# Transposing put-off probabilities two trios at a time, and filling TensorE's early gaps for longer

## The chip, the cores and the metric

The kernel runs on one core of one Trainium2 chip. The metric is the device time of one execution in microseconds (us). It ran three times before the change; the median is the time before. A profile of one further execution gives the trace: the start and length of every instruction on each engine, and the clock that was granted to TensorE.

## The reference

Two layers, one after the other, in float32. First, causal attention with a sliding window of 128 positions and a linear distance bias, for 8 batches and 8 heads of 576 positions and 64 features; then a gated feed-forward layer over all 4608 tokens.

```python
scores = scale * np.matmul(q, k.transpose(0, 1, 3, 2))
mask = (rel >= 0) & (rel < window)          # rel: query position - key position
scores = np.where(mask, scores + bias[None], -1000000000.0)
scores = scores - np.max(scores, axis=-1, keepdims=True)
attn = np.exp(scores)
attn = attn / (np.sum(attn, axis=-1, keepdims=True) + 1e-09)
out = np.matmul(attn, v)
...
gate = 1.0 / (1.0 + np.exp(-(x @ w_gate)))   # x: 4608 x 512, w_gate: 512 x 1536
val = x @ w_val
return gate * val @ w_out                    # 1536 x 512
```

## The kernel before, in words

**Stages.** From 0 to about 296 us the kernel computes attention and, mixed into it, the gate and value products of the first 3072 tokens for four of the twelve feature chunks ("the stream", line 659). From 296 to about 700 us come the other gate and value products (line 793), and after that the output product (line 927).

**Units, blocks, runs, trios.** Attention is cut into 32 units, each a batch and a pair of heads. A unit has nine blocks of 128 rows. `scores` (line 430 and after) takes a run of eight blocks (four in the first units), which may straddle two units. Its matmuls (line 459) write score banks in PSUM. VectorE then puts masked parts in place (476) and does bias and row minimum (484), and ACT the exponentials with their sums (488). Three blocks make a trio. `probabilities` finishes a trio: POOL adds the small constant to the sums (561), VectorE takes reciprocals (563), VectorE or ACT scale the three blocks (566, 567), TensorE transposes them (573) into one of two work banks, ACT or VectorE copy that bank out (205, 206), and POOL makes two selections out of it into the unit's tile `pt` (584).

**What is put off.** For units from the ninth on (`VHEAD`), a trio that ends in a run isn't finished there: it goes on the list `put_off` and is handed to `probabilities`, one trio after the other, in the next run, behind that run's scores. A run leaves two or three trios. `split_values` multiplies `pt` with the values (line 530) in two halves, one ahead of a run's scores and one behind; both halves use both work banks (`WORK`, banks 6 and 7), and copies out of them to `xt` follow. `work()` hands out the two work banks by turns.

**The order of the work.** Every piece is put into a graph with its engine, a cost, what it reads and writes, and a due time (`want`). `Graph.order` then plans all engines: of the pieces whose inputs are planned, it takes the one that can start first; between equal starts, the one that is due first. The stream has a due time of a million, so it goes wherever nothing else can start. Each engine then has its instructions in planned order, for good. The planner charges LAT on top of a cost before a result may be used (0.25 for TensorE, 0.2 for ACT), SLACK 0.1 ahead of put-off transposes, SWITCH / 2 = 0.18 where TensorE changes the kind of matmul, and STAY 0.4 for leaving attention's kind after time 30.

**Fillers.** Where the plan leaves TensorE idle before time `WARM`, the planner notes how many filler matmuls fit, and `warm` (line 290) multiplies the identity with itself that often, into a bank that nothing reads then. Each filler is two matmul records in the trace.

```python
if o.eng == "PE" and o.start < WARM:
    gap = (o.start - free["PE"] - 0.2) // (0.25 if free["PE"] > 5.0 else 0.45)
```

## Time and profile before

| what | value |
|---|---|
| median of 3 runs | 963.4 us (963.06 to 966.7) |
| the profiled execution | 963.38 us |
| its span, first to last instruction | 961.6 us |
| mean granted TensorE clock | 0.998 |
| TensorE busy in the span | 954.6 us, 6634 matmuls |
| transposes, line 573 | 288 matmuls, 216 + 36 + 36 in three groups |
| fillers, line 290 | 62 matmuls, 10.1 us |
| stream, line 659 | 576 matmuls, 157.1 us |

The profile names engines PE (TensorE matmuls), PEld (its weight loads), DVE (VectorE), ACT (ScalarE), POOL (GpSimd) and SP (which starts DMAs). L573 is line 573 of the kernel before. Matmuls are pipelined, so the length of one overlaps that of the next; distances between starts, and the chain of waits, tell what a group costs. A row of the timeline gives start, length, engine, line, operation, tiles and count, and in brackets the idle time before it with what ended it. A row of the chain gives start, length, and what. A row of windows gives the window and its length, then busy time and number of instructions for PE, PEld, DVE, ACT and POOL, and at the end the granted clock, the DMA share and GB/s.

### The profile page before, as it was taken

The numbers are of one execution on the slowest core, as the hardware profiler recorded it, in microseconds if no ns is written. First come the engines' busy times: TensorE is split into PE (matmuls) and PEld (weight loads), VectorE is DVE, ScalarE is ACT, GpSimd is POOL, SyncE is SP. The second block draws the span as 40 slices with busy tenths as digits, with TensorE's granted clock in tenths as the row PEclk, the third lists the DMA queues.
The fourth block names the chain that finished last, engine by engine and source line by source line (L and its number), as shares of the span: only waits on it lengthen the run. The fifth ranks groups of instructions, "written<-read, shape, count | busy, mean of one in ns | idle before, by whom it ended". The sixth has DMA issues, their size and how long they took to land.

```text
span 961.6 us, 18712 instructions
## 1 busy us (share of the span) xinstructions
PE 954.6 (99%) x6634; PEld 833.6 (87%) x6634; DVE 763.8 (79%) x1893; ACT 517.7 (54%) x1341; POOL 143.2 (15%) x316
## 2 busy tenths in 40 slices
PE   9999999999999999999999999999999999999998
PEld 7678888888889999999988888888888888889998
DVE  8999788788898899878976775674597878877783
ACT  8998788878876354434533543442343433333341
POOL 3545345444441000000000000000000000000000
PEclk9999999999999999999999999999999999999999
DMA  8787778867654344335573473379856254352601
GB/s 308 262 285 251 239 250 290 283 203 244 230 198 163 121 153 136 101 143 192 182 286 116 155 284 134 140 288 347 311 190 207 100 169 159 96 167 88 189 25 50
DMA packets 82653, 186.03 MB, mean 193 GB/s; under 512 B 7808, under 2 KB 36864, under 8 KB 82560
## 3 DMA queue, kind: packets, MB, share of 16 engines
q1 hardware_dynamic: 82416, 184.71, 56.3%
q8 instruction: 52, 0.85, 0.4%
q14 instruction: 41, 0.34, 0.1%
q10 hardware_dynamic: 144, 0.13, 0.1%
HBM read 121.90 MB, written 62.91 MB: 192 GB/s over the span
## 4 chain that ended last, share of the span: by engine, by line
PE 97%; DVE 2%; ACT 0%; issue 0%; POOL 0%; POOLq 0%; DVEq 0%
PE mm L793 42%; PE mm L927 27%; PE mm L659 15%; PE mm L459 5%; PE mm L530 4%; PE mm L573 3%; PE mm L611 1%; PE mm L290 1%; DVE pb L484 0%; DVE pb L566 0%; DVE mm L476 0%; ACT pb L488 0%; DVE first L214 0%; DVE wbits L352 0%; DVE st L563 0%
## 5 line engine op out<-in xcount | busy, mean ns | idle before, releaser
L793 PE MATMUL mm<-xc,w2s 128*128 128x384 f32 (+1 forms) x2016 | 403.8, 362 | 0.0
L793 PEld LDWEIGHTS mm<-xc,w2s 128*128 128x128 f32 x2016 | 363.7, 188 | 39.7 <-DVE later_hs L800 0.5
L927 PE MATMUL mm<-duo,wo 128*128 128x512 f32 (+1 forms) x1260 | 258.9, 367 | 0.0
L927 PEld LDWEIGHTS mm<-duo,wo 128*128 128x128 f32 x1260 | 229.4, 188 | 29.5
L659 PE MATMUL mm<-first,first 128*128 128x512 f32 x576 | 157.1, 409 | 0.1
L659 PEld LDWEIGHTS mm<-first,first 128*128 128x128 f32 x576 | 101.9, 190 | 21.5 <-issue 1.1
L804 ACT ACTIVATE sg<-mm 128x384 f32<-128x384 f32 (+1 forms) x96 | 52.2, 545 | 111.5 <-PE mm L793 63.1
L800 DVE TENSOR_TENSOR mm<-mm,low 128x384 f32<-128x384 f32 (+1 forms) x96 | 60.3, 629 | 60.9 <-PE mm L793 60.1
L205 ACT COPY low<-mm 128x512 f32<-128x512 f32 (+1 forms) x93 | 49.6, 536 | 78.5 <-PE mm L793 66.7
L488 ACT ACTIVATE pb<-pb,st 128x128 f32<-128x128 f32 x216 | 84.6, 397 | 2.1 <-DVE st L484 1.9
L584 POOL TENSOR_SCALAR_AFFINE_SELECT pt<-early_h 128x384 f32<-128x384 f32 x96 | 51.3, 553 | 57.0 <-ACT early_h L205 56.6
L584 POOL TENSOR_SCALAR_AFFINE_SELECT pt<-spread 128x384 f32<-128x384 f32 x96 | 52.3, 567 | 44.0 <-ACT spread L205 43.7
L476 DVE COPY_PREDICATED mm<-early_h,mm 128x256 f32<-128x256 int32 (+1 forms) x144 | 48.8, 389 | 4.1 <-PE mm L459 4.1
L530 PEld LDWEIGHTS mm<-pt,vr 64*64 64x64 f32 x1056 | 43.1, 133 | 10.0 <-issue 5.0
L484 DVE CUSTOM_DVE_ANT_0 pb<-mm,early_h 128x128 f32<-128x128 f32 x216 | 49.6, 282 | 0.0
L530 PE MATMUL mm<-pt,vr 64*64 64x192 f32 (+2 forms) x1056 | 47.3, 284 | 0.0
L566 DVE TENSOR_SCALAR pb<-pb,st 128x128 f32<-128x128 f32 x169 | 42.1, 296 | 1.3
L488 ACT ACTIVATION_READ_ACCUMULATOR pb<-pb,st 128x1 f32 x216 | 41.8, 193 | 0.0
L808 DVE SCALAR_TENSOR_TENSOR later_hs<-sg,later_hs 128x384 f32<-128x384 f32 (+1 forms) x48 | 30.1, 628 | 13.8 <-ACT sg L804 13.6
L205 ACT CAST duo<-csum 128x1024 fp32r<-128x1024 f32 (+1 forms) x26 | 25.2, 969 | 29.0 <-PE mm L927 13.2
L205 ACT COPY early_h<-mm 128x384 f32<-128x384 f32 (+3 forms) x75 | 32.1, 444 | 14.0 <-PE mm L530 8.6
L800 DVE TENSOR_TENSOR later_hs<-mm,later_hs 128x384 f32<-128x384 f32 (+1 forms) x48 | 29.8, 620 | 11.9 <-ACT sg L804 6.5
(144 smaller groups left out, 1202.0 us busy)
## 6 DMA issues: line engine op xcount, KB each, us to landing
hid<-later_hs SPq DMA_DIRECT2D x24, 512.0 KB, 3.8
wo<-stash_o SPq DMA_DIRECT2D x12, 896.0 KB, 7.4
vr<-in_v_dram SPq DMA_DIRECT2D x32, 288.0 KB, 5.0
hid<-later_hs SPq DMA_DIRECT2D x24, 384.0 KB, 2.9
stash_o<-wtmp SPq DMA_DIRECT2D x12, 768.0 KB, 3.5
wraw<-in_moe_w_gate_dram SPq DMA_DIRECT2D x14, 512.0 KB, 5.0
wraw<-in_moe_w_val_dram SPq DMA_DIRECT2D x14, 512.0 KB, 4.1
kr<-in_k_dram SPq DMA_DIRECT2D x11, 576.0 KB, 5.1
```

Of the source, the lines that this page charges most:

```text
L205: g.add("ACT", act_cost(n, psum), lambda: nc.scalar.copy(out(), src()), reads, writes, want, release=release, slack=slack, ways=[("DVE", d ...
L459: nc.tensor.matmul(to, qraw(u)[rows, i // 2, h * D:(h + 1) * D], keys, start=True, stop=True)
L476: g.add("DVE", dve_cost((a1 - a0) * P, psum=True), lambda b=b, a0=a0, a1=a1: nc.vector.copy_predicated(quads(b)[:, a0:a1, 1:3], before[:, ...
L484: g.add("DVE", 0.21, lambda: nc.vector.tensor_tensor_reduce(pb()[:, e], sp[b][:, a, D:D + P], relm[u.p][:, w], op0=ALU.add, op1=ALU.min, s ...
L488: g.add("ACT", 0.39, lambda: nc.scalar.activation(pb()[:, e], pb()[:, e], AF.Exp, bias=st()[:, e:e + 1], scale=-1.0, accum_out=st()[:, 3 + ...
L530: nc.tensor.matmul(mm[WORK[h]][e * D:(e + 1) * D, a - e * S - cuts[h]:b - e * S - cuts[h]], vraw(u)[r * D:r * D + D, c], seen, start=first ...
L584: nc.gpsimd.affine_select(pt(u)[:, f0:f0 + 2 * n - 1:2, :], both(), [[0, n], step], cmp, 0.0, base=0, channel_multiplier=mult)
L659: nc.tensor.matmul(mm[s][:, 0:wd], w.tile(kind, wi, i)[:, c * P:(c + 1) * P], xpart(x, c)[:, 0:wd], start=(k == 0 and c == 0), stop=(k == ...
L793: nc.tensor.matmul(mm[b][:, 0:N2], w.tile2(i, wp)[:, wk, c * P:(c + 1) * P], combo(k, xp, N2)[:, c], start=(start and c == 0 and j == 0), ...
L800: g.add("DVE", dve_cost(N2, psum=True), lambda: nc.vector.tensor_tensor(o(), bk(b)(), a(), op=ALU.add), [("mm", b), *reads] if okeys else ...
L804: g.add("ACT", act_cost(N2, psum=True), lambda: nc.scalar.activation(sg[h](), bk(b)(), AF.Tanh, scale=0.5), [("mm", b)], [("sg", h)], F)
L927: nc.tensor.matmul(mm[b][:, 0:N2], wo2(2 * q + m, wp)[:, k, j * P:(j + 1) * P], duo(xp)[:, m], start=(k in (0, 3, 1) and q == 0 and m == 0 ...
```

## The change

Two edits. First, `probabilities` takes a list of trios. Put-off trios are handed to it two at a time (a third one alone). For each trio the sums, reciprocals and scaling are put into the graph as before; then there is one TensorE piece for all transposes of the list, which reads all its scaled blocks and writes one work bank per trio, so for two trios both of them; its due time is that of the first trio. Then come the copy and the two selections of each trio. Trios that aren't put off go through the same function alone. Second, the time limit `WARM` of the fillers goes from 30 to 45, and they also end with the first matmul of the stream; the limit of 30 in STAY's condition stays, now called `EAGER`.

```diff
--- before.py
+++ after.py
@@ -60,7 +60,7 @@
 W1, WSTEP1 = 0.0, 6.0
 WW, WWSTEP = 28.0, 2.0
 SWITCH = 0.36
-WARM = 30.0
+EAGER, WARM = 30.0, 45.0
 LATE = 4.0
 LATEX = 0.0
 LAND = 4.0
@@ -122,6 +122,7 @@
         free["PE"] = 1.5
         wait = []
         port = moved = 0.0
+        streams = False
         mode = 0
         for o in self.ops:
             if not o.left:
@@ -134,7 +135,7 @@
                 for k, way in enumerate(o.ways):
                     e, cost, lat, shared, emit = way
                     s = max(free[e], o.ready, port if shared else 0.0)
-                    leave = STAY if e == "PE" and mode == 1 and o.mode != 1 and s > WARM else 0.0
+                    leave = STAY if e == "PE" and mode == 1 and o.mode != 1 and s > EAGER else 0.0
                     key = (s + cost - least + leave + (YIELD[e] if k else 0.0), o.want, o.seq)
                     if best is None or key < best[0]:
                         best = key, o, way, s
@@ -142,7 +143,8 @@
             if o.eng == "PE" and o.mode != mode:
                 mode = o.mode
                 o.start += SWITCH / 2
-            if o.eng == "PE" and o.start < WARM:
+            streams = streams or o.eng == "PE" and o.want == 1.0e6
+            if o.eng == "PE" and o.start < WARM and not streams:
                 gap = (o.start - free["PE"] - 0.2) // (0.25 if free["PE"] > 5.0 else 0.45)
                 if gap > 0:
                     self.fill.append((free["PE"] + 0.01, int(gap)))
@@ -468,7 +470,8 @@
         g.add("PE", cost, matmuls, reads, writes, want, slack=0.0 if pend else slack, release=release, mode=1)
         then()
         while put_off:
-            probabilities(*put_off.pop(0))
+            probabilities(put_off[:2])
+            del put_off[:2]
         for b, on in sorted(used.items(), key=lambda kv: blks.index(kv[1][0][:2])):
             a = [a for u, i, a in on if i]
             if a:
@@ -493,7 +496,7 @@
                 if u.n >= VHEAD and blks.index((u, i)) >= len(blks) - VLATE:
                     put_off.append((u, i - TRI + 1))
                 else:
-                    probabilities(u, i - TRI + 1)
+                    probabilities([(u, i - TRI + 1)])
             if i == VDELAY * TRI - 1 and 0 < u.n <= VHEAD:
                 done(units[u.n - 1])
 
@@ -552,41 +555,41 @@
                 load(units[u.n + NSLOT], False)
         return then
 
-    def probabilities(u, i0):
-        m, _, st, pb, kst, kpb = three_of(u, i0)
-        want = u.when(i0 + TRI)
-        slack = 0.0 if u.n < HEAD else SLACK
-        n, kb = TRI, ("both", m % NBOTH)
-        both = lambda: spread2[m % NBOTH]
-        g.add("POOL", 0.2, lambda: nc.gpsimd.tensor_tensor(st()[:, 6:9], st()[:, 3:6], little, op=ALU.add),
-              [(kst, 3 + e) for e in range(n)], [(kst, 6)], want, port=False)
-        g.add("DVE", 0.09, lambda: nc.vector.reciprocal(st()[:, 6:9], st()[:, 6:9]), [], [(kst, 6)], want)
-        for e in range(n):
-            args = lambda e=e: (pb()[:, e], pb()[:, e], st()[:, 6 + e:7 + e])
-            g.add("DVE", 0.19, lambda args=args: nc.vector.tensor_scalar_mul(*args()), [(kst, 6)], [(kpb, e)], want, port=True,
-                  ways=[("ACT", 0.3, False, lambda args=args: nc.scalar.mul(*args()))])
-
-        z = work()
+    def probabilities(trios):
+        n, turn, behind = TRI, [], []
+        for u, i0 in trios:
+            m, _, st, pb, kst, kpb = three_of(u, i0)
+            want = u.when(i0 + TRI)
+            kb = ("both", m % NBOTH)
+            both = lambda m=m: spread2[m % NBOTH]
+            g.add("POOL", 0.2, lambda st=st: nc.gpsimd.tensor_tensor(st()[:, 6:9], st()[:, 3:6], little, op=ALU.add),
+                  [(kst, 3 + e) for e in range(n)], [(kst, 6)], want, port=False)
+            g.add("DVE", 0.09, lambda st=st: nc.vector.reciprocal(st()[:, 6:9], st()[:, 6:9]), [], [(kst, 6)], want)
+            for e in range(n):
+                args = lambda e=e, pb=pb, st=st: (pb()[:, e], pb()[:, e], st()[:, 6 + e:7 + e])
+                g.add("DVE", 0.19, lambda args=args: nc.vector.tensor_scalar_mul(*args()), [(kst, 6)], [(kpb, e)], want, port=True,
+                      ways=[("ACT", 0.3, False, lambda args=args: nc.scalar.mul(*args()))])
+            turn.append((work(), pb, kpb))
+            behind.append((u, i0, want, kb, both))
 
         def transpose():
-            for e in range(n):
-                nc.tensor.transpose(mm[z][:, e * P:(e + 1) * P], pb()[:, e], ident)
-
-        g.add("PE", 0.095 * n, transpose, [(kpb, e) for e in range(n)], [("mm", z)], want, slack=slack)
-        copy(lambda: both(), lambda: mm[z][:, 0:n * P].rearrange("p (a q) -> p a q", a=n), n * P, [("mm", z)], [kb], want, psum=True)
-        for own in range(2):
-            step, cmp, mult = ([1, P], ALU.is_ge, -1) if own else ([-1, P], ALU.is_gt, 1)
-
-
-
-            def spread(own=own, step=step, cmp=cmp, mult=mult):
-                f0 = 2 * i0 + own
-                nc.gpsimd.affine_select(pt(u)[:, f0:f0 + 2 * n - 1:2, :], both(), [[0, n], step], cmp, 0.0,
-                                        base=0, channel_multiplier=mult)
-
-            g.add("POOL", 0.13 + 0.12 * n, spread, [kb], [("pt", u.n % NPT, i0 + e, own) for e in range(n)], want)
-
-
+            for z, pb, _ in turn:
+                for e in range(n):
+                    nc.tensor.transpose(mm[z][:, e * P:(e + 1) * P], pb()[:, e], ident)
+
+        g.add("PE", 0.095 * n * len(turn), transpose, [(kpb, e) for _, _, kpb in turn for e in range(n)], [("mm", z) for z, _, _ in turn],
+              behind[0][2], slack=0.0 if trios[0][0].n < HEAD else SLACK)
+        for (z, _, _), (u, i0, want, kb, both) in zip(turn, behind):
+            copy(both, lambda z=z: mm[z][:, 0:n * P].rearrange("p (a q) -> p a q", a=n), n * P, [("mm", z)], [kb], want, psum=True)
+            for own in range(2):
+                step, cmp, mult = ([1, P], ALU.is_ge, -1) if own else ([-1, P], ALU.is_gt, 1)
+
+                def spread(u=u, i0=i0, both=both, own=own, step=step, cmp=cmp, mult=mult):
+                    f0 = 2 * i0 + own
+                    nc.gpsimd.affine_select(pt(u)[:, f0:f0 + 2 * n - 1:2, :], both(), [[0, n], step], cmp, 0.0,
+                                            base=0, channel_multiplier=mult)
+
+                g.add("POOL", 0.13 + 0.12 * n, spread, [kb], [("pt", u.n % NPT, i0 + e, own) for e in range(n)], want)
 
     def values(u):
         want = u.when(NBLK + 1)
@@ -986,7 +989,7 @@
                     prepare(w1, src, kind, i, WW + WWSTEP * (k - len(todo) // 2), W1 + WSTEP1 * (k - len(todo) // 2))
         first_pass()
     while put_off:
-        probabilities(*put_off.pop(0))
+        probabilities([put_off.pop(0)])
     for _, u in pend:
         split_values(u, u.when(NBLK + 1), [], [], 0.0)()
     first_pass()
```

## The prediction

> **What bounds the kernel now.** I read the page first: its totals and its chain of work that ended last.

> ```profile
> span 961.6 us, 18712 instructions
> PE 954.6 (99%) x6634; PEld 833.6 (87%) x6634; DVE 763.8 (79%) x1893; ACT 517.7 (54%) x1341; POOL 143.2 (15%) x316
> PE 97%; DVE 2%; ACT 0%; issue 0%; POOL 0%; POOLq 0%; DVEq 0%
> ```

> TensorE is the bound nearly everywhere. The change touches the first stage only (attention, mixed with the first product stream, up to 296 us). The view by windows, cut there, shows how much idle time is left to win (after the window: its length, then PE busy):

> ```profile
> 100.00:200.00 100.00, 99.90 (x1260) 84.26 (x1259) 81.79 (x403) 80.56 (x315) 42.46 (x102) 1.00 0.82 273
> 200.00:296.00 96.00, 96.00 (x1060) 79.82 (x1060) 81.90 (x348) 73.96 (x272) 41.16 (x91) 1.00 0.62 207
> 34.53:37.95 3.42, 1.93 (x23) 1.14 (x23) 3.42 (x19) 3.29 (x13) 2.32 (x6) 1.00 0.86 325
> 37.95:41.36 3.41, 3.41 (x17) 2.81 (x14) 3.41 (x16) 2.50 (x10) 0.82 (x2) 0.50 0.85 275
> 17.47:20.88 3.41, 3.04 (x34) 2.37 (x34) 3.20 (x21) 3.41 (x17) 1.56 (x5) 1.00 0.72 252
> ```

> From 100 to 296 us only 0.1 us is idle: in a dense stretch, shortening a wait wins nothing, and a new wait costs its whole length. The one weak place is at 35 us: TensorE is busy for 1.93 of 3.42 us, and in the next 3.41 us the granted clock is 0.50. A window with 3.04 us busy (17.47) was not followed by that.

> **The pair itself, on TensorE.** One run of eight score blocks, in the chain (start, length, what):

> ```profile
> 138.04 0.90 PE mm L659 x3
> 138.94 0.66 PE mm L573 x6
> 139.60 0.69 PE mm L659 x3
> 140.28 0.33 PE mm L573 x3
> ```

> Line 573 is the transposes, 659 the stream. The planner already puts two trios side by side: six transposes, three stream matmuls, three transposes. Six cost 0.66 us and three cost 0.33, so joining removes no seam that the chain can show; all 288 transposes stay. I bound this gain by 0 and, at 0.02 us for each of 27 pairs, 0.5 us, and take -0.3.

> [...]

> **The pair, in the planner's order.** Here is the possible loss. After a run's scores come the second half of the split values (L530), two copies out of the two work banks on ACT, and the transposes, which need those banks:

> ```profile
> 137.00 1.04 PE L530 MATMUL mm<-pt,vr 64*64 64x192 f32 x22
> 138.78 0.82 PE L573 MATMUL mm<-ident,pb 128*128 128x128 f32 x6
> 138.08 0.70 ACT L205 COPY early_h<-mm 128x320 f32<-128x320 f32 x2 [0.32 <-PE mm L530]
> 142.44 1.60 POOL L584 TENSOR_SCALAR_AFFINE_SELECT pt<-early_h 128x384 f32<-128x384 f32 x2 [0.58 <-ACT early_h L205]
> 144.66 0.92 PE L530 MATMUL mm<-pt,vr 64*64 64x192 f32 x21
> ```

> Counted by the planner's own charges (they fix only the order) from the start of the second values half: it ends at 0.71; the copies may start at 0.96 and end at 1.28 and 1.54; with ACT's 0.2 and SLACK 0.1 the first bank is usable at 1.58 and the second at 1.84. One stream step of three matmuls ends at 0.71 + 0.18 + 0.69 = 1.58. So today the first trio starts just there, and the second follows when its bank is due. A pair is ready only at 1.84, the planner takes what can start first, and a second stream step slips in: both trios one step later, priced by the 0.69 us of the chain row above. Behind them on TensorE wait the stream and the next scores; behind their result, two copies, four POOL selections, and the next values (144.66), which wait for the last selection, ended at 142.44 + 1.60 = 144.04. That is 0.62 us before. I compared, in 22 runs from 85 to 271 us, the start of the values with the last selection that had ended; it was 0.69 us or less in 15 (first row of the run at 85.27 and last of the one at 260.06):

> ```profile
> 84.58 0.99 POOL L584 TENSOR_SCALAR_AFFINE_SELECT pt<-spread 128x384 f32<-128x384 f32 x2 [0.74 <-ACT spread L205]
> ...
> 258.72 1.23 POOL L584 TENSOR_SCALAR_AFFINE_SELECT pt<-early_h 128x384 f32<-128x384 f32 x2
> ```

> In those 15 the next run starts a stream step later. That alone leaves TensorE dense, since stream work is done meanwhile: 15 x 0.69 = 10.4 us of it earlier. The bill comes at the end of the stage, where attention's last chain runs under what is left of the stream (groups from 273.7 to 295.9 us; then waits from 280 to 296 us):

> ```profile
> L659 PE MATMUL mm<-first,first 128*128 128x512 f32 x69 | 17.9, 403 | 0.0
> L530 PE MATMUL mm<-pt,vr 64*64 64x192 f32 (+2 forms) x88 | 3.9, 288 | 0.0
> ...
> ACT sg L670 <- PE mm L659: 2.2, 2, 1.8
> ACT xc L205 <- PE mm L659: 2.2, 2, 1.5
> ```

> 69 matmuls are 23 steps, 15.9 us at 0.69. With 15 steps gone, 10.4 of the 22.2 us are uncovered. Against that: the chain shrinks where ACT waited for the stream, 2.2 + 2.2 = 4.4 us; and the next stage can lend products, because its first combination is made at 281.7 us though L793 starts at 295.96:

> ```profile
> 280.72 0.96 DVE L214 TENSOR_TENSOR xc<-later_xr,xc 128x768 fp32r<-128x768 f32 x1 [0.29 <-ACT xc L205]
> ...
> 295.96 403.69 PE mm L793 x2016
> ```

> At 403.69 / 2016 = 0.20 us a matmul, a product of six is 1.2 us; I take two or three, 3 us (an estimate from these rows). 10.4 - 4.4 - 3.0 = 3.0 us of idle time. Bounds: no slip in any run, 0; all 22 runs slip, 22 x 0.69 = 15.2, less 7.4, is 7.8 us, and an idle tail can bring a half-clock stretch as at 38 us, 3.41 / 2 = 1.7 more: 9.5. I take 3.0, nearer to the low end, because the 15 is counted and the ends are not.

> Moved with each late run go its stores to xs and loads on SP's queue. They have room late in the stage; the one place where the stream now runs dry is here, and a later store could lengthen it by tenths, inside the bounds above.

> ```profile
> 133.41 0.70 DVE early_hs L678
> ```

> VectorE, ACT and POOL get the same instructions. Where the second trio's scaling is planned ahead of the first's transposes, nothing is added.

> **The filler matmuls.** The limit for filling planned gaps goes from 30 to 45, until the stream's first matmul. On the chip:

> ```profile
> 7.39 2.05 PE L290 MATMUL mm<-ident 128*128 128x128 f32 x16
> 29.19 0.71 PE L290 MATMUL mm<-ident 128*128 128x128 f32 x4
> 34.11 0.55 PE L573 MATMUL mm<-ident,pb 128*128 128x128 f32 x3
> 35.27 0.54 PE L459 MATMUL mm<-early_h,early_xr 64*64 64x192 f32 x2 [0.61 <-DVE st L484]
> 36.68 0.39 PE L459 MATMUL mm<-early_h,early_xr 64*64 64x192 f32 x3 [0.88 <-DVE st L484]
> 39.55 2.46 PE L659 MATMUL mm<-first,first 128*128 128x512 f32 x6
> ```

> The last filler now is at 29.19 and the first stream matmul at 39.55; between them is a gap of about 2 us ahead of the scores at 36.68 (0.61 and 0.88 idle, 0.54 of two early matmuls). The rule in the code gives (2.0 - 0.2) // 0.25 = 7 fillers, 14 records, at 2.05 / 16 = 0.13 us about 1.8 us. They lie under VectorE's L484, which ends the wait at 36.68; uncovered they would cost those 1.8 us, on the path at most 0.2. Busy time in the window at 34.53 becomes about 3.4 us, above the 3.04 that kept the clock, so the half-clock stretch should go. Its price, by the chain: (slow first, the same work at full clock below)

> ```profile
> 37.56 1.50 PE mm L611 x9
> 39.06 0.83 PE mm L573 x3
> 39.90 2.12 PE mm L659 x6
> ...
> 51.65 1.40 PE mm L659 x6
> 55.39 1.02 PE mm L611 x9
> 56.41 0.48 PE mm L573 x3
> ```

> 0.48 + 0.35 + 0.72 = 1.55 us. VectorE has no idle time there (3.41 of 3.41), so not all of it can come through: from 0 to -1.55, taken at -1.1.

> [...]

> **Sum.** -0.3 + 3.0 - 1.1 = +1.6 us. The profiled execution took 963.38 us (961.6 of span, 1.8 around it), which is the median of the runs, 963.4. Forecast 965.0, own range 962.5 to 967.5.

> **Rivals.**
> - The pair changes no gate (the second copy goes to VectorE, or the tail absorbs the steps). For it: the pairs stand side by side already, and in 7 of 22 runs there was over 0.69 us of room. Against it: 15 had none. 963.4 - 0.3 - 1.1 = 962.0.
> - The stream is used up early and the tail is bare. Place: TensorE from about 274 to 300 us, waiting for POOL and ACT. It decides from about 11 steps pulled ahead (7.4 / 0.69), and at 20 or more it exceeds 6 us, with the half clock on top. For it: a bank that is 0.26 late in the planner's count is late in every run alike. Against it: runs gated by VectorE's score reductions do not move. 963.4 - 1.4 + 9.0 = 971.0.
> - The fillers don't lift the clock (too few, or elsewhere), while the tail is as forecast: 965.0 + 1.1 = 966.1.

> **Chances.** Forecast 0.40, no gate moved 0.30, bare tail 0.20, fillers without effect 0.10. About 0.5%, 4.8 us, is what a measurement of this kernel can tell from no change: 958.6 to 968.2. Faster than that would need more idle time than the stage has: 0.03. Slower: the bare tail, and the edge of the forecast, 0.22. Same: 0.75. The range runs from the first rival less its scatter, 960.8, to the second's centre, 971.0.

> **What would show it.** Right: 14 more L290 records near 34.7 us and a granted clock of 1.00 at 38 to 41 us; after the values, six stream matmuls before six transposes; fewer than 69 stream matmuls after the last scores, and idle TensorE near the end of the stage. Wrong: still three stream matmuls before the six (then the second rival falls and 962 is right), or TensorE idle before transposes in mid-stage, which no step here forecasts.

## The result, and the profile after

The changed kernel takes 968.65 us (968.43 to 969.43, six runs), the kernel before 963.32 us (six runs, the three earlier ones among them). By these medians it is 5.3 us (0.55%) slower; the ratio over the runs is 1.0062, interval 1.0053 to 1.0072, and the whole interval lies above the 0.5% that was called no change. The profiled executions took 968.73 and 963.38 us. Three executions with a mean granted clock of 0.85 or less (1060.5 us and more, one of the late trios below and two of the kernel before) are left out of all times and counts here.

Lines have moved: 573, 659, 793, 530, 459 and 290 of the kernel before are 578, 662, 796, 533, 461 and 292 of the changed one (one or a few lines off in the experiments). First the changed kernel's page and its view by windows, in stretches from 60 us on, with one early window:

```profile
span 967.0 us, 18720 instructions
PE 956.3 (99%) x6648; PEld 834.6 (86%) x6648; DVE 763.3 (79%) x1883; ACT 521.7 (54%) x1352; POOL 142.7 (15%) x315
...
60.00:284.00 224.00, 223.79 (x2539) 186.75 (x2531) 186.46 (x841) 175.51 (x664) 92.53 (x212) 1.00 0.74 246
284.00:310.00 26.00, 21.62 (x246) 18.90 (x245) 21.40 (x76) 18.82 (x64) 9.18 (x22) 1.00 0.26 91
310.00:400.00 90.00, 89.37 (x513) 88.44 (x512) 83.97 (x146) 43.30 (x84) 4.47 (x3) 1.00 0.44 145
37.35:40.76 3.41, 3.41 (x33) 2.74 (x31) 3.41 (x16) 3.30 (x11) 1.47 (x2) 1.00 0.81 267
```

The same three late windows of the kernel before:

```profile
60.00:284.00 224.00, 223.90 (x2623) 187.09 (x2622) 191.17 (x904) 184.01 (x706) 97.54 (x226) 1.00 0.75 247
284.00:310.00 26.00, 26.00 (x208) 23.17 (x207) 22.70 (x38) 15.56 (x30) 5.71 (x7) 1.00 0.51 170
310.00:400.00 90.00, 90.00 (x521) 89.98 (x520) 83.40 (x147) 40.75 (x81) 3.63 (x5) 1.00 0.40 128
```

TensorE is busy for 956.3 us of 967.0, so the span has 10.7 us without it, where the old one had 7.0. Read the first number after the window's length (TensorE busy), and the second (its weight loads). Up to 284 us the changed kernel is as dense as the old one: 0.21 us idle against 0.10. From 284 to 310 us it idles for 4.38 us, where the old one has none. From 310 to 400 us its weight loads miss 1.56 us, the old one's 0.02: in the second stage, which no line of the change touches. From 37.35 us on, where the old kernel ran at half clock, the clock is 1.00.

What the pair does in the middle of the stage, and what is left at its end (timeline of TensorE, changed kernel):

```profile
34.09 1.73 PE L292 MATMUL mm<-ident 128*128 128x128 f32 x14
...
139.80 1.67 PE L662 MATMUL mm<-first,first 128*128 128x512 f32 x6
141.30 0.82 PE L578 MATMUL mm<-ident,pb 128*128 128x128 f32 x6
...
282.70 2.31 PE L662 MATMUL mm<-first,first 128*128 128x512 f32 x9
284.85 1.23 PE L796 MATMUL mm<-xc,w2s 128*128 128x384 f32 x6
286.82 1.46 PE L461 MATMUL mm<-kr,qr 64*64 64x192 f32 x29
288.31 0.98 PE L533 MATMUL mm<-pt,vr 64*64 64x192 f32 x22
290.25 0.87 PE L578 MATMUL mm<-ident,pb 128*128 128x128 f32 x6 [0.95 <-ACT xt L207]
291.71 1.32 PE L796 MATMUL mm<-xc,w2s 128*128 128x384 f32 x6 [0.59 <-DVE st L487]
293.11 2.36 PE L796 MATMUL mm<-xc,w2s 128*128 128x384 f32 x12
295.56 1.84 PE L578 MATMUL mm<-ident,pb 128*128 128x128 f32 x9
298.43 0.97 PE L533 MATMUL mm<-pt,vr 64*64 64x192 f32 x22 [1.03 <-ACT early_h L207]
299.72 0.98 PE L533 MATMUL mm<-pt,vr 64*64 64x192 f32 x22 [0.32 <-DVE turn L542]
301.27 1.10 PE L533 MATMUL mm<-pt,vr 64*64 64x192 f32 x22 [0.56 <-issue]
303.06 0.98 PE L533 MATMUL mm<-pt,vr 64*64 64x192 f32 x22 [0.69 <-ACT turn L542]
303.97 1.31 PE L796 MATMUL mm<-xc,w2s 128*128 128x384 f32 x6
```

The end of the same stage in the kernel before:

```profile
271.49 1.46 PE L459 MATMUL mm<-kr,qr 64*64 64x192 f32 x29
273.60 0.73 PE L659 MATMUL mm<-first,first 128*128 128x512 f32 x2
294.07 0.98 PE L659 MATMUL mm<-first,first 128*128 128x512 f32 x3
294.98 0.98 PE L530 MATMUL mm<-pt,vr 64*64 64x192 f32 x22
295.89 1.31 PE L793 MATMUL mm<-xc,w2s 128*128 128x384 f32 x6
```

In the changed kernel six stream matmuls stand ahead of the six transposes (141.30); so it is in 18 of the 24 runs of six from 60 to 284 us that follow the stream, with more than six in five others. In the kernel before it was three in 21 of 22. The last scores start at 286.82 instead of 271.49. The last stream matmuls run at 282.70, ahead of those scores; 69 came behind them before. What is left between 288 and 304 us is attention's own chain, with a hole ahead of most of its steps, and 18 products borrowed from the next stage (6 at 291.71, 12 at 293.11), after six more at 284.85. The last values start 8.1 us later (303.06 against 294.98).

### The profile page after: what moved, and what is told of

It reads as the page before. It is cut to its first block, busy times and chain, and to the rows that moved or that the text cites. A ratio compares the mean times of both kernels' runs of the same rounds, so it can differ in the third digit from the quotient of the medians.

```text
span 967.0 us, 18720 instructions
## 1 busy us (share of the span) xinstructions
PE 956.3 (99%) x6648; PEld 834.6 (86%) x6648; DVE 763.3 (79%) x1883; ACT 521.7 (54%) x1352; POOL 142.7 (15%) x315
## 4 chain that ended last, share of the span: by engine, by line
PE 94%; DVE 3%; ACT 2%; POOL 1%; issue 1%; DVEq 0%; ACTq 0%; POOLq 0%
PE mm L796 41%; PE mm L930 27%; PE mm L662 13%; PE mm L461 5%; PE mm L533 3%; PE mm L578 3%; PE mm L614 2%; PE mm L292 1%; ACT pb L491 1%; POOL pt L589 1%; DVE mm L479 0%; DVE pb L570 0%; DVE w2s L216 0%; ACT early_h L207 0%; ACT spread L207 0%
## 5 line engine op out<-in xcount | busy, mean ns | idle before, releaser
L662 PE MATMUL mm<-first,first 128*128 128x512 f32 x576 | 153.0, 406 | 0.0
L207 ACT COPY early_h<-mm 128x384 f32<-128x384 f32 (+3 forms) x70 | 29.7, 442 | 14.3 <-PE mm L533 11.1
```

The source lines that it names most:

```text
L207: g.add("ACT", act_cost(n, psum), lambda: nc.scalar.copy(out(), src()), reads, writes, want, release=release, slack=slack, ways=[("DVE", d ...
L662: nc.tensor.matmul(mm[s][:, 0:wd], w.tile(kind, wi, i)[:, c * P:(c + 1) * P], xpart(x, c)[:, 0:wd], start=(k == 0 and c == 0), stop=(k == ...
```

## The experiments

The kernel before was timed beside each of their three series: 962.77, 963.17 and 963.09 us. So a few tenths between kernels of different series say nothing. Two theories were to be told apart first. By the slip, the joint piece is planned later than the first trio alone was, a stream step gets ahead in each run, attention ends later, and the stream isn't there any more to cover its end. By the pair as such, the cost lies in the joint piece: six transposes at once, or both work banks held together.

**Fillers alone.** The kernel before, with the second edit only.

```diff
-WARM = 30.0
+EAGER, WARM = 30.0, 45.0
...
+            streams = streams or o.eng == "PE" and o.want == 1.0e6
-            if o.eng == "PE" and o.start < WARM:
+            if o.eng == "PE" and o.start < WARM and not streams:
```

> The fillers alone: the limit of 45 that ends with the stream, trios one after the other as before. Slip theory (the pair's loss comes from one more stream step ahead of it): 14 more filler records near 34 us, a granted clock of 1.00 from 38 to 41 us, the same order of attention as before, 1.5 to 1.9 us less than before: 961.4 to 961.8. Rival (VectorE bounds that stretch, so what the clock gives is waited away by 60 us): as before, 963.3.

Measured: 962.4 us (961.56 to 962.61), ratio 0.9996 (0.9987 to 1.0005), between the two forecasts. The median hides two values of the kernel before. Its 51 runs of the three series fall apart by the mean granted clock of the run:

| kernel before, mean clock | runs | median us |
|---|---|---|
| 0.998 | 28 | 963.2 |
| 1.0 | 23 | 962.0 |

The difference, 1.2 us, fits the half-clock stretch that the profile showed at 38 us; a stretch of 3.41 us at half clock is also what takes a mean of 1.0 to 0.998 (1.7 / 962). None of the eleven runs with fillers is below 0.999. So the fillers do prevent the stretch, which is worth 1.2 us in some half of the executions. Against the old kernel's executions without it they are 0.4 us slower (962.4 against 962.0); in the trace, weight loads miss 0.49 us from 310 to 400 us, where the old ones miss 0.02. By the median nothing is left that can be told from nothing. In the later kernels with the same fillers some runs stand at 0.998 again (8 of all 69 runs with fillers); none of those was profiled, so where their clock fell is open.

**Pairs alone.** The changed kernel, fillers as before.

```diff
-EAGER, WARM = 30.0, 45.0
+EAGER, WARM = 30.0, 30.0
...
-            if o.eng == "PE" and o.start < WARM and not streams:
+            if o.eng == "PE" and o.start < WARM:
```

> The pair alone: the changed kernel with the fillers' limit back at 30. Slip theory: the half clock is back at 38 us, the bare tail stays: 968.65 plus 1.5 to 1.9, 970.2 to 970.6. Rival (the fillers are worth nothing by the end): 968.65.

Measured: 970.07 us (968.63 to 973.72), ratio 1.0080 (1.0064 to 1.0096), 0.13 us below the forecast. The whole loss is the pair's: two of the six runs have a mean clock of 1.0, and their 968.63 and 968.81 us are the changed kernel's time. The two slowest (971.73 and 973.72 us) have 0.996 and 0.993, more than one such stretch can make; they weren't profiled. This kernel's profiled execution (968.81 us) had the same two gaps as the kernel before, and no half clock (windows, then the timeline of TensorE, kernel with pairs alone):

```profile
31.96:35.37 3.41, 2.80 (x35) 1.83 (x30) 3.41 (x17) 3.38 (x11) 1.28 (x3) 1.00 0.94 341
35.37:38.78 3.41, 2.53 (x32) 1.84 (x31) 3.41 (x14) 3.28 (x14) 1.74 (x4) 1.00 0.84 278
34.00:37.40 3.40, 1.91 (x21) 1.06 (x23) 3.40 (x20) 3.27 (x12) 2.66 (x6) 1.00 0.96 352
...
35.09 0.54 PE L461 MATMUL mm<-early_h,early_xr 64*64 64x192 f32 x2 [0.61 <-DVE st L487]
36.50 0.39 PE L461 MATMUL mm<-early_h,early_xr 64*64 64x192 f32 x3 [0.88 <-DVE st L487]
```

In the kernel before, the trace's record of full clock begins at 7.23 us and lasts 30.72 us, the record of half clock 3.413 us, and the next one of full clock 921.60 us: 9, 1 and 270 steps of 3.413. Laid out in such steps, one window, 34.53 to 37.95 us with 1.93 us busy, held both gaps, and the clock fell at its end. In the kernel with pairs alone, laid out as in the first two rows, one gap falls into each stretch, 2.80 and 2.53 us are busy, and the clock stays at 1.00, although the stretch from 34.00 to 37.40 us has both gaps and only 1.91 us busy. That fits a share of busy time counted in windows whose place against the program differs from run to run, and the two values of the table above; it is the author's reading, and no row shows where the windows of that kernel begin.

**Late trios, not joined.** Fillers alone, and each put-off trio transposed by itself; the first two are planned 0.27 later, about as late as the pair.

```diff
-        while put_off:
-            probabilities(*put_off.pop(0))
+        for k in range(len(put_off)):
+            probabilities(*put_off.pop(0), late=0.27 if k < 2 else 0.0)
...
-        g.add("PE", 0.095 * n, transpose, [(kpb, e) for e in range(n)], [("mm", z)], want, slack=slack)
+        g.add("PE", 0.095 * n, transpose, [(kpb, e) for e in range(n)], [("mm", z)], want, slack=slack + late)
```

> No pairs: the kernel of before with the new fillers, in which the first two put-off trios of a run get 0.27 more planned slack, so that each is planned one stream step later, one after the other, each with its own wait and its own bank. Slip theory: six stream matmuls ahead of the first transposes in most runs, the stream nearly used up at the last scores, several us of idle TensorE in the tail: 966 to 968.7. Rival (it is the joint piece, six transposes that hold both banks under one wait, that costs): as with fillers alone, 961.6.

Measured: 967.71 us (966.5 to 968.49), ratio 1.0049 (1.0036 to 1.0062): 5.3 us over the fillers alone, where the pair is 6.25 over them. Timeline of TensorE, late trios:

```profile
138.45 1.66 PE L661 MATMUL mm<-first,first 128*128 128x512 f32 x6
139.95 0.82 PE L575 MATMUL mm<-ident,pb 128*128 128x128 f32 x6
...
296.41 0.97 PE L532 MATMUL mm<-pt,vr 64*64 64x192 f32 x22 [0.62 <-ACT early_h L207]
298.05 0.98 PE L532 MATMUL mm<-pt,vr 64*64 64x192 f32 x22 [0.66 <-ACT turn L541]
300.46 1.10 PE L532 MATMUL mm<-pt,vr 64*64 64x192 f32 x22 [1.43 <-issue]
```

The same six stream matmuls ahead, holes at the end again, and no joint piece: being planned later is enough for most of the loss. The stream is not used up here, though it was expected to be nearly so: 30 of its matmuls still come behind the last scores.

**The pair planned earlier.** The joint piece is put ahead by a slack of -0.2 where it has two trios.

```diff
-              behind[0][2], slack=0.0 if trios[0][0].n < HEAD else SLACK)
+              behind[0][2], slack=-0.2 if len(trios) > 1 else 0.0 if trios[0][0].n < HEAD else SLACK)
```

> Pairs kept, the slip taken away: for a pair the planned slack is -0.2 in place of 0.1, so that the planner puts it behind one stream step as it did the two single trios; on the chip it still waits for both banks and all six blocks. Slip theory: three stream matmuls ahead of the six transposes in most runs, most of the 69 stream matmuls still there after the last scores: 961.5 to 964.5. Rival (joint piece): 968 to 969, or waits of TensorE ahead of the pairs that add up to as much.

Measured: 966.75 us (965.94 to 968.09), ratio 1.0044 (1.0032 to 1.0056). A miss for both forecasts. Attention does end earlier (60 stream matmuls are left behind the last scores, and the end is covered), but there are new waits inside the stage (waits and timeline, pair at -0.2):

```profile
PE mm L578 <- ACT early_h L207: 1.8, 1, 1.8
PE mm L796 <- ACT sg L807: 1.2, 1, 1.2
...
266.52 1.79 DVE L354 SCALAR_TENSOR_TENSOR wbits<-wraw,wbits 128x512 int32<-128x512 int32 x1
268.49 0.40 ACT L571 ACTIVATE kept<-kept,st 128x128 f32<-128x128 f32 x1 [2.73 <-DVE st L567]
269.53 0.55 PE L578 MATMUL mm<-ident,early_h 128*128 128x128 f32 x3 [1.78 <-ACT early_h L207]
```

VectorE is 1.79 us in a piece of weight preparation; ACT waits 2.73 us for the reciprocals behind it, and the copies for which TensorE waits stand behind that scaling.

**Earlier still:** the same edit with -0.4.

> As the early pair, with a planned slack of -0.4: another plan without the slip, so that the one wait of 1.8 us at 268 us, which ended the early pair's gain, should not be met again at that place. Slip theory: three stream matmuls ahead of the six in most runs, 55 or more stream matmuls after the last scores, no bare tail: below the early pair's 966.75, 963 to 965.5. Rival (a joint piece costs by itself, about 4 us over the fillers alone, wherever it is planned): 966.5 to 968.5.

Measured: 964.26 us (963.75 to 966.75), ratio 1.0015 (1.0006 to 1.0024), the best with pairs in all of the stage. Three stream matmuls stand ahead of the pair again (timeline, pair at -0.4):

```profile
144.58 0.97 PE L662 MATMUL mm<-first,first 128*128 128x512 f32 x3
145.39 0.55 PE L578 MATMUL mm<-ident,early_h 128*128 128x128 f32 x3
145.78 0.49 PE L578 MATMUL mm<-ident,kept 128*128 128x128 f32 x3
```

66 stream matmuls are left behind the last scores, and no hole is at the end. It is still 1.9 us over the fillers alone. Of that, about 1.0 is found at the joint piece itself: over the 24 pairs from 80 to 284 us the first two transposes start 136.9 ns apart (108.5 before), and the first follows the stream by 248.4 ns (233.9). In the changed kernel, with its later pair, these stand at 108.4 and 232.6. That the piece is now issued before both banks and blocks are ready fits this; no wait in the trace is long enough to show it.

**Half of the stage.** Pairs only for units below 20, and only from 20 on.

```diff
-            probabilities(put_off[:2])
-            del put_off[:2]
+            k = 2 if u0.n < 20 else 1
+            probabilities(put_off[:k])
+            del put_off[:k]
```

> Pairs only in runs that begin before unit 20, single trios after it; fillers as in the changed kernel. Slip theory with a threshold (the first 11 or so steps that are pulled ahead cost nothing, since the last chain of attention has stream work to lie under): 7 to 12 steps pulled ahead, more than 30 stream matmuls left after the last scores, no idle TensorE in the tail above 1 us: 962.4 to 964. Rival (each slipped step costs its share, 6.3 us / 23 steps): 964.5 to 965.5.

> Pairs only in runs that begin at unit 20 or later, single trios before. Slip theory with a threshold: as the first half, 962.4 to 964, because only the sum of the steps counts. Rival 1 (each step costs its share): 964.3 to 965.3. Rival 2 (it is the late pairs next to the tail that cost, not the sum): 967 or more, while the first half is free.

Measured: 964.47 us (964.0 to 964.83), ratio 1.0013 (1.0004 to 1.0022), with pairs in the first half; 967.0 us (966.86 to 967.28), ratio 1.0039 (1.0026 to 1.0051), in the second. Over the fillers alone that is 2.1 and 4.6 us, in sum 6.7 against 6.25 for all pairs, so there is no number of free steps before the price begins. No forecast holds for both halves: the threshold misses both, the equal share fits the first half to 0.03 us and misses the second, and the late pairs alone, which fit the second, would leave the first half free. The second half leaves 48 stream matmuls and no hole in the tail, and pays in the next stage (windows and waits, pairs in the second half):

```profile
310.00:400.00 90.00, 87.43 (x497) 85.60 (x496) 82.28 (x143) 40.56 (x80) 4.74 (x4) 1.00 0.43 142
PE mm L797 <- ACT low L207: 1.4, 2, 0.8
PE mm L797 <- DVE later_hs L804: 0.8, 1, 0.8
PE mm L797 <- DVE xc L216: 0.3, 1, 0.3
```

**Late trios in half of the stage.** The same halves with unjoined late trios.

```diff
+            probabilities(*put_off.pop(0), late=0.27 if k < 2 and u0.n < 20 else 0.0)
```

> Single trios, the first two of a run planned one step later (0.27 more slack) only in runs that begin before unit 20; fillers as in the changed kernel. If the time follows from how late attention ends, whatever made it late: the planner lets the stream run dry twice in mid-stage here (about 132 and 211 us) and attention catches up, so the last values end 0 to 3 us after those of the fillers alone: 962.4 to 965. If the place of the slips counts and not the end: as pairs in the first half, 964.5, with the last values 5 us later.

> The same, only in runs that begin at unit 20 or later, no pairs anywhere. If it is the slip: like pairs in the second half, the last values 6 to 9 us later than with the fillers alone, idle time in the tail or waits of the next stage's products, 966 to 968. If pairs as such are the cost: 962.4 to 963.

Measured: 966.15 us (965.53 to 967.42), ratio 1.0033 (1.0023 to 1.0044), for the first half, above all that was expected; 965.15 us (964.91 to 967.23), ratio 1.0024 (1.0014 to 1.0034), for the second, between the two forecasts. The first pays inside the stage, where TensorE waits (waits, late trios in the first half):

```profile
PE mm L532 <- POOL pt L586: 1.5, 2, 1.2
PE mm L661 <- DVE early_hs L680: 0.5, 1, 0.5
```

Two of these three waits stand at 216 to 218 us, ahead of values whose selections come late, and one at 263.5, where the stream's next combination isn't made yet. The second pays in the tail, in three holes of 0.32, 0.56 and 1.20 us ahead of the last values, and in one wait of 0.6 us in the next stage. So which half costs more depends on where a wait opens. The last values start 4.4 and 5.8 us later than with the fillers alone, where 0 to 3 and 6 to 9 were forecast from the end of attention. The two halves together, 6.5 us over the fillers alone, are more than the whole, 5.3.

| kernel | us | over fillers alone | PE idle 60–284 | 284–310 | weight loads idle 310–400 |
|---|---|---|---|---|---|
| fillers alone | 962.4 | 0 | 0.10 | 0 | 0.49 |
| changed | 968.65 | 6.25 | 0.21 | 4.38 | 1.56 |
| late trios | 967.71 | 5.3 | 0.03 | 2.72 | 1.45 |
| late trios, first half | 966.15 | 3.75 | 2.08 | 0 | 0.17 |
| late trios, second half | 965.15 | 2.75 | 0.10 | 2.08 | 1.58 |
| pairs, first half | 964.47 | 2.1 | 0.08 | 0.25 | 1.46 |
| pairs, second half | 967.0 | 4.6 | 0.12 | 0 | 4.40 |
| pairs at -0.2 | 966.75 | 4.35 | 1.78 | 0 | 1.54 |
| pairs at -0.4 | 964.26 | 1.9 | 0.18 | 0 | 0.32 |

The last three columns are each window's length less its busy time, from the view by windows of each kernel. Less the 0.59 of the fillers alone, their sum comes to within 2.1 us of the loss in every row, so they show the places and not the whole size; for late trios in the first half that remainder is more than half of the loss, and for pairs at -0.4 all of it. What is left counts as busy, and no row says what it is. How late attention ends goes with the loss, but not strictly: against the fillers alone the last values start 9.7 and 9.4 us later in the changed kernel and with late trios, 7.5 with pairs in the second half, 4.4 to 5.8 in the other halves and with pairs at -0.2, and 0.9 with pairs at -0.4. No version with pairs beats the kernel before, and none of the nine beats it by more than can be told from nothing.

## Why the prediction was right or wrong

Forecast 965.0, measured 968.65: slower, as forecast, but outside the forecast's own range (up to 967.5), between it and the second rival (971.0). That it would be slower by more than 0.5% had been given 0.22. By its steps:

- **The pair itself, on TensorE (-0.3): nothing won, nothing lost.** Within a run of six, transposes follow each other at 108 to 109 ns in both kernels, and TensorE hardly waits ahead of them: 0.21 us idle in 224. No run shows the 0.02 us a pair that the -0.3 was made from; it was the author's estimate. The clock is 1.00 in that window in both kernels.
- **The pair in the planner's order: right in mechanism.** Six stream matmuls stand ahead of six transposes, as forecast, and late trios without a joint piece lose 5.3 us over the fillers alone, where the pairs lose 6.25.
- **Fifteen slipping runs: the term that was mis-sized.** The last scores start 15.3 us later, in a kernel that was 1.9 us ahead at 60 us (the scores at 61.02 in the chain of before start at 59.15). These 17.2 us are 25 steps of 0.69, and all 23 steps that covered the tail were pulled ahead. The count had taken a run to slip only where its values followed the last selection within 0.69 us. But the changed kernel's order is planned anew: where a gate looked loose in one trace, the run was put later all the same.
- **The tail (+3.0): 5.7 measured at the seam.** The 25th product of the next stage starts at 300.16 us before and at 303.97 after, 3.8 later, and with the 1.9 us by which the kernel was ahead that is 5.7. Of it 4.4 are the idle TensorE that was forecast. The other 1.3 fit how idle time is counted: the view counts it from the end of the matmul before, and in a dense stretch the next one starts ahead of that end (transposes are 0.29 us long from 288 to 304 us, and start 0.11 apart in a run of six). Reckoned from start to start against the dense stretches of before, the ten gaps from 60 to 304 us cost about 6 us, where the view shows 4.6 (an estimate from the traces). Both credits were too small: from the last scores to the last values it takes 16.2 us instead of 23.5, so the chain shrank by 7.2 us where 4.4 were taken, and 24 products were lent, 4.8 us at the prediction's 0.20, where it took 3. With 23 steps in place of 15 its own sum then gives 15.9 - 7.2 - 4.8 = 3.9, near the 4.4 that were idle. So a count that was too low and credits that were too low worked against each other, and that the 3.0 was not further off is luck. The half clock of the upper bound did not come: the clock is 1.00 from 284 to 400 us. So the second rival had the place and the number of steps (over 20), and at 9.0 too high a price.
- **No term for the next stage.** The product stream ends 5.35 us later (699.65 by the chain of before, 371.75 + 333.25 = 705.00 by the row below), so 1.5 us more are lost behind the seam. The prediction let the slip end with attention. That weight preparation and evictions on VectorE and ACT, held up behind a late attention, pass it on is argued, not shown: in the changed kernel one wait of 0.6 us, for an eviction, is all that the view names. It stands out most with pairs in the second half, whose tail has no hole at all and whose next stage loses most, with waits for evictions on ACT and VectorE and once for the combination (`xc`).
- **The fillers (-1.1): about right against the execution that was profiled.** There are 14 more records, the clock is whole, the first stream matmul comes 1.15 us earlier, and 1.2 us lie between the two values of the kernel before. At 60 us the changed kernel is 1.9 us ahead, more than the 1.55 that was given as the most; with the fillers alone the profiled execution ends 1.0 us ahead (962.4 against 963.38). But 23 of 51 executions have no half-clock stretch to repair, and the sum was made against one that has.

Against the profiled execution the account is 5.7 + 1.5 - 1.9 = +5.3 us, as measured. The chain of the changed kernel (start, length, what), and four of TensorE's eight kinds of wait from 60 to 720 us (total, times, longest), of which the kernel before has none:

```profile
371.75 333.25 PE mm L796 x1608
...
PE mm L533 <- ACT early_h L207: 1.0, 1, 1.0
PE mm L578 <- ACT xt L207: 1.0, 1, 1.0
PE mm L533 <- ACT turn L542: 0.7, 1, 0.7
PE mm L796 <- DVE later_hs L803: 0.6, 1, 0.6
```

The last row is the next stage's wait. The first rival (no gate moved, 962.0) falls with the six stream matmuls at 139.80, the third (fillers without effect) with the clock of 1.00 at 37.35.

## What to carry to other kernels

Where an order is planned and then fixed, a piece that may start 0.26 us later can let a step of other work ahead of it in nearly every place where it stands, and the price comes where that other work runs out or in a wait that the new plan opens: look where the filling stream ends, charge every step of the slip against what is left of it there, and look one stage further for preparation that was pushed back. Where a median is made of executions with and without a dip of the clock, a repair of the dip is worth, in the mean, its price times the share of executions that have it.
